# Second feed-forward product by seven half products, with the gated products parked in device memory

## The chip, the cores and the metric

The kernel runs on one core of one Trainium2 chip. The metric is device microseconds of one execution, and a smaller number is better. The engines are named as in the profile: PE is TensorE (matmuls), DVE is VectorE, ACT is ScalarE, POOL is GpSimd, and SP is SyncE, whose queue issues nearly all transfers. SBUF is the core's memory, PSUM holds matmul results in eight banks, and device memory is outside the core.

## What is computed

The reference is causal attention over 4 batches, 12 heads, 448 positions and 64 dimensions; then a layer with 4 attention experts of which each position mixes two; then a feed-forward block with a convolution gate. The last one is what the change touches:

```
h = np.maximum(x @ w_in, 0.0)                     # 4 x 448 x 1024
conv_out = sum over k of conv_w[k] * h shifted by k - 1
gate = 1.0 / (1.0 + np.exp(-conv_out))
return (h * gate) @ w_out                         # w_out: 1024 x 768
```

All values are float32.

## The kernel before

The feature dimension lies on the 128 partitions and the 448 positions of a batch lie in a row. A product keeps float32 accuracy by splitting both operands into a high part and the rest (a low part) and adding three passes: high x high, high x low, low x high (`PASSES`, line 24). So each operand of a product costs a copy (high) and a subtraction (low) ahead of it.

The program is written as tasks with needs, buffers and alternative engines (`Program.add`, line 135). `ORDER` (line 28) is a packed table: for each step it gives a task's number and the engine that runs it. `Program.run` (line 191) walks that table, so the table sets the order of the instructions on each engine. Where the table's planner expected PE to wait for long, `warm` (line 1314) puts small matmuls on the identity.

Four stages follow one another and overlap. `attend` (line 561) makes the first attention by pairs of heads (tiles `sk_A`, `P_A`, `PT_A`) and writes `xT` (lines 786 to 798). `proj_qk` and `proj_v` (lines 937 and 983) project it for the experts, and `attend` runs again with names in M. Both write `oc` to device memory (line 779). Meanwhile `fold_all` (line 834) folds the experts' output weights into w_in, giving `wp`, and `wout_convert` (line 1090) takes w_out, which comes as raw 64-bit words, to float32 (`from_f64`, line 395) and splits it: twelve steps of 512 columns, whose parts are saved to device memory.

`ffn_batch` (line 1145) loads `oc` of one batch, splits it on POOL (lines 1161 to 1171), and runs, for each of 8 chunks of 128 features, the first product (line 1188, 6 matmuls), relu on ACT (1201), three taps of the convolution (ACT at 1207, DVE at 1209 twice), tanh on ACT (1215), the gate's product on DVE (1219), and the split of the result into high (ACT, 1223) and low (DVE, 1226). The result stays in PSUM until it is split, and the parts `g` stay in SBUF.

`ffn_out` (line 1240) makes one block of 128 output features of one batch: 8 chunks x 3 matmuls (line 1251) into one bank, one evacuation by ACT or DVE (1261) and one store (1265). There are 6 blocks and 4 batches. A block may begin as soon as its batch's first chunks are split.

Of the kernel before, what the change touches and what calls it, by code (L numbers as in the profile page):

```python
# [33 lines left out]
    "z#{}aj)uF%q3{Ge4G$7N5&)u(2ofLTpWsXQCHxwG1OFG{Gl5Hlh(&M(d;z`$H^E)-5d4#}PoWa7!4KdC;VS_`nTTHEG37_n6OtO7BfTJP;kWTd"
    "0!(-dZW7DH3eiFE5)`Nm;hcyjT@nw7zfs;&b|@A60sa{OE9n(!gY=G6A)S*BNB|ioQi*+p5Mh9D1S)HEH6w&cLV*w>evi_k?8Fo?OT16KBt0aK"
    "5w3|-gd)LQGea(s$50${9yN^u$tA)NY8Leq^BHr1I6<5tZj$GTFPJZx+r%Rxo<t*YNEVWwq$16drKIP?CGsBmh$JRIA(qLDgjIrpZDc#x=aehT"
    "GLcGNA>L9BnODqX<~2z{M#zL(sFqfH!*r4&q<&J4lp=Xa+vFAUKDkIfCfmtCjh{Wv&a=<R%WPCFTzkr7*M1@6DFt?v>?d2uY4RX>i2R!QhFNB!"
    "DRb-vc9}iJUS%V-rrJ>LI5|&VXK%CrC5({9NO@A0{GM5;U9O$0y(7~pY>K_sS+i9uq39@k?1S2!+5>hG^@V*@yIQ+myHM+^F;Nth7(2th$0pQ#"
# [79 lines left out]
class Program:  # L118
# [64 lines left out]
    def idle_bank(self, since):  # L183

        for kinds in self.banks.values():
            for k in kinds:
                o = self.owner.get(k)
                if o is None or (o.left == 0 and o.ready <= since):
                    return k
# [75 lines left out]
def attn_moe_ffn_kernel(  # L265
# [1119 lines left out]
```

## Time and profile before

| | |
|---|---|
| median of 3 runs | 504.17 us (500.73 to 504.58) |
| the profiled execution's own time | 503.03 us |
| its span, first to last instruction | 501.2 us |
| PE, DVE, ACT, POOL busy | 97%, 74%, 70%, 52% of the span |
| matmul instructions in the page | 3202 |
| moved by DMA | 73.03 MB, 146 GB/s on average |

The page gives the busy time of each engine over the span. How busy an engine was in a stage is read from the table of stretches, what ended the wait of an engine from the table of waits, and what stands one behind the other up to the end from the chain. The duration of one instruction is in the groups by line and shape; matmul durations overlap with their neighbours, so the time from one matmul to the next is taken from the chain.

### The profile page before, as it was taken

Reading aid. Unit: us, or ns where it says so; the run is one execution under the profiler, and the core shown is the slowest. Engines: PE = TensorE matmul, PEld = TensorE weight load, DVE = VectorE, ACT = ScalarE, POOL = GpSimd, SP = SyncE. Lnnn points to the kernel's source line nnn. Section 1 sums busy time; section 2 is a strip of 40 time slices with the busy share of each in tenths; the row PEclk is TensorE's granted clock in tenths of the full one; section 3 lists DMA queues with packets and bytes.
Section 4 is the critical chain, followed back from the end, with each engine's and each line's share of the span. In section 5 each row is a group of like instructions: output and inputs, shape, how many; then the busy total and the mean of one; then the engine's idle time right before and its main releaser. Section 6 shows DMA issues by size and latency. Waiting matters only on the chain.

```text
span 501.2 us, 9905 instructions
## 1 busy us (share of the span) xinstructions
PE 487.5 (97%) x3202; PEld 419.7 (84%) x3202; DVE 369.0 (74%) x1110; ACT 349.8 (70%) x970; POOL 261.9 (52%) x388
## 2 busy tenths in 40 slices
PE   8788999999999999999999999999999999999997
PEld 6656878988888898888988788898999989999996
DVE  4999999988899686987789984487587556374300
ACT  5989999998889768886888893386566554344201
POOL 1856879978879777998788944162022002000000
PEclk9999999999999999999999999999999999999999
DMA  8857468996793767665688615838220112101011
GB/s 216 211 164 186 128 179 225 232 250 192 203 242 106 178 173 214 142 176 136 202 204 237 151 57 168 272 148 213 88 90 0 56 37 80 51 16 58 37 38 73
DMA packets 29171, 73.03 MB, mean 146 GB/s; under 512 B 4160, under 2 KB 11072, under 8 KB 28352
## 3 DMA queue, kind: packets, MB, share of 16 engines
q1 hardware_dynamic: 29040, 72.18, 51.8%
q8 instruction: 25, 0.41, 0.4%
q10 hardware_dynamic: 80, 0.23, 0.2%
q14 instruction: 26, 0.21, 0.1%
HBM read 50.50 MB, written 13.63 MB: 128 GB/s over the span
## 4 chain that ended last, share of the span: by engine, by line
PE 74%; DVE 11%; POOL 5%; DMA 4%; issue 2%; ACT 1%; SPq 0%; POOLq 0%; DVEq 0%; ACTq 0%
PE bank L1251 23%; PE bank L952 9%; PE bank L690 9%; PE bank L760 9%; PE bank L637 9%; PE bank L1188 8%; PE bank L998 4%; DMA nat<-in_qk_dram 4%; DVE P_A L650 3%; PE bank L881 3%; POOL sk_A L340 2%; DVE PT_A L337 1%; POOL P_M L333 1%; POOL P_A L333 1%; DMA cwraw<-in_conv_w_dram 1%
## 5 line engine op out<-in xcount | busy, mean ns | idle before, releaser
L1251 PE MATMUL bank<-g,wout 128*128 128x448 f32 x576 | 123.2, 367 | 0.0
L1251 PEld LDWEIGHTS bank<-g,wout 128*128 128x128 f32 x576 | 107.4, 188 | 8.8
L659 ACT ACTIVATE P_A<-P_A,nm_A 112x448 f32<-112x448 f32 (+3 forms) x192 | 99.4, 521 | 15.7 <-DVE nm_A L650 10.4
L340 POOL TENSOR_TENSOR sk_A<-nat,sk_A 64x448 fp32r<-64x448 f32 (+1 forms) x77 | 90.3, 1172 | 9.7 <-ACT sk_A L331 3.9
L650 DVE CUSTOM_DVE_ANT_0 P_A<-bank,mask 112x448 f32<-112x448 f32 (+3 forms) x192 | 80.0, 440 | 10.8 <-PE bank L595 6.3
L637 PE MATMUL bank<-sk_A 128*112 128x112 f32 (+3 forms) x352 | 66.4, 312 | 3.5 <-DVE nm_A L650 2.9
L952 PE MATMUL bank<-xT,wqk 128*128 128x448 f32 x288 | 68.7, 374 | 0.6 <-DVE sk_M L968 0.4
L690 PE MATMUL bank<-ident,P_A 112*112 112x112 f32 x480 | 61.7, 264 | 3.3 <-DVE xT L792 1.4
L333 POOL TENSOR_SCALAR P_A<-P_A,r_A 112x336 f32<-112x336 f32 (+3 forms) x97 | 49.9, 526 | 25.7 <-DVE r_A L670 9.2
L637 PEld LDWEIGHTS bank<-sk_A 128*112 128x112 f32 x352 | 48.8, 176 | 10.1 <-DVE nm_A L650 4.5
L690 PEld LDWEIGHTS bank<-ident,P_A 112*112 112x112 f32 x480 | 49.8, 135 | 8.0 <-DVE xT L792 1.6
L952 PEld LDWEIGHTS bank<-xT,wqk 128*128 128x128 f32 x288 | 51.2, 188 | 4.1 <-DVE sk_M L968 0.5
L1209 DVE SCALAR_TENSOR_TENSOR bank<-h,cw,bank 128x448 f32<-128x448 f32 x64 | 43.5, 687 | 14.8 <-ACT bank L1207 11.6
L760 PE MATMUL bank<-PT_A,v 112*64 112x448 f32 (+3 forms) x384 | 50.4, 406 | 0.1
L760 PEld LDWEIGHTS bank<-PT_A,v 112*64 112x64 f32 x384 | 26.2, 137 | 23.6 <-issue 12.3
L331 ACT ACTIVATE P_A<-P_A,r_A 112x448 f32<-112x448 f32 (+3 forms) x87 | 42.3, 517 | 4.6 <-DVE r_A L670 4.3
L1188 PE MATMUL bank<-ocs,wp 128*128 128x448 f32 x192 | 43.5, 367 | 0.0
L998 PE MATMUL bank<-wvg,xT 128*112 128x260 f32 x288 | 41.2, 287 | 0.2 <-DVE wm L434 0.2
L333 POOL TENSOR_SCALAR sk_A<-nat 128x896 fp32r<-128x896 f32 x35 | 33.0, 941 | 12.6 <-DMA nat<-in_qk_dram 11.6
L1188 PEld LDWEIGHTS bank<-ocs,wp 128*128 128x128 f32 x192 | 35.7, 188 | 3.0
L659 ACT ACTIVATE P_M<-P_M,nm_M 112x224 f32<-112x224 f32 (+3 forms) x64 | 33.3, 522 | 6.8 <-DVE nm_M L650 5.3
L331 ACT ACTIVATE PT_A<-bank 112x336 f32<-112x336 f32 (+1 forms) x75 | 33.9, 472 | 5.2 <-PE bank L690 5.0
(105 smaller groups left out, 820.2 us busy)
## 6 DMA issues: line engine op xcount, KB each, us to landing
nat<-in_qk_dram SPq DMA_DIRECT2D x88, 224.0 KB, 4.0
wraw<-in_w_in_dram SPq DMA_DIRECT2D x12, 512.0 KB, 5.5
woraw<-in_w_out_dram SPq DMA_DIRECT2D x12, 512.0 KB, 5.1
wo<-wohl SPq DMA_DIRECT2D x12, 512.0 KB, 4.1
wout<-wo SPq DMA_DIRECT2D x6, 1024.0 KB, 10.0
v<-in_v_dram SPq DMA_DIRECT2D x24, 224.0 KB, 4.5
out_dram<-osb SPq DMA_DIRECT2D x24, 224.0 KB, 1.9
sk_M<-sk_M SPq DMA_DIRECT2D x16, 224.0 KB, 4.2
```

Of the source, the lines that this page charges most:

```text
L331: nc.scalar.activation(dst, src, AF.Copy, scale=scale)
L333: nc.gpsimd.tensor_scalar(dst, src, scale, 1.0 if scale2 is None else scale2, ALU.mult, ALU.mult)
L340: (nc.gpsimd if e == "POOL" else nc.vector).tensor_tensor(dst, a, b, op)
L637: nc.tensor.matmul(sp[:CP], t[:, j.o[h], m * CP : (m + 1) * CP], t[:, j.o[h] + k, :w], start=(k == 2), stop=(k == 1),)
L650: nc.vector.tensor_tensor_reduce(rows(i), st["s", i][:CP, :w], mask[:, S - w :], -SCALE, 3.0e38, ALU.add, ALU.min, st["nm"][:, i : i + 1],)
L659: nc.scalar.activation(rows(i), rows(i), AF.Exp, bias=st["nm"][:, i : i + 1], scale=-1.0, accum_out=st["sm"][:, i, 0:1],)
L690: nc.tensor.transpose(pt[:CP, o : o + CP], rows(i)[:, kt * CP : (kt + 1) * CP], ident[:CP, :CP])
L760: nc.tensor.matmul(st["ov"][h * D : (h + 1) * D, kt * CP : S], j.v[:, kt, h, :], j.PT[h][:, col_base[kt] : col_base[kt] + S - kt * CP], st ...
L952: nc.tensor.matmul(st["ps"][:, :S], proj["wqk"][:, a, cc, w, p * P : (p + 1) * P], xT[b, cc][:, b2, :], start=(cc == 0 and (a, b2) == PASS ...
L998: nc.tensor.matmul(st[i][:CP, :VW], xT[b, cc][:, a, i * CP : (i + 1) * CP], proj["wvg"][:, b2, cc, :], start=(cc == 0 and (a, b2) == PASSE ...
L1188: nc.tensor.matmul(st["ps", c][:, :S], wp[:, a, ec, c * P : (c + 1) * P], st["oc", ec][:, b2], start=(ec == 0 and (a, b2) == PASSES[0]), s ...
L1251: nc.tensor.matmul(st["ps"][:, :S], ffn["wout", n][:, a, c], gs[c][:, b2], start=(c == 0 and (a, b2) == PASSES[0]), stop=(c == NFC - 1 and ...
```

## The change

Two batches are treated as the two halves of columns of one product, the two halves of w_out's rows (4 chunks each) and of its output features (3 blocks each) are the other halves, and the 2 x 2 half product is made with seven half products in place of eight. What changes in the code:

- `wout_convert` takes six steps, each with a block of w_out's upper and of its lower output half. It makes four sums and differences (`combine`), and saves seven sets of split half-size weights. `wset_load` loads them, 1.5 MB each.
- `ffn_batch` no longer splits the gated product. DVE writes it to SBUF in float32 (`mul`), and `park` stores it to device memory. The factor of one half of the gate goes into relu.
- `chunk_operands` loads the two chunks of a half of both batches of a pair back, makes four differences, and splits seven operands into high and low parts, on the engine that the table names.
- `ffn_out` runs once for a pair of batches: seven products of 3 blocks x 4 chunks x 3 matmuls. `ffn_sum` adds each result to what `SUMS` names: a running sum in SBUF or a quarter of the output, which is then stored.
- The space comes from tiles that the attention leaves (`unit_space`, `HOMES`): names that begin with `ux`, `us`, `uv`, `up` and `uq` are such tiles; "u" slots hold split operands, "w" slots loaded chunks, "d" slots differences and running sums.
- `ORDER` is a new table for the whole program.

```diff
-    BANKS = dict(s=(0, 1, 4), t=(2, 3, 5), v=(4, 5), m=(6, 7), h=(6, 7, 0, 2), o=(5, 3, 1))
+    BANKS = dict(
+        s=(0, 1, 4), t=(2, 3, 5), v=(4, 5), m=(6, 7), h=(6, 7, 0, 2), o=(5, 3, 1, 4, 2, 0),
...
+    PRODUCTS = ((0, "b11"), (1, "b21"), (2, "t2"), (4, "t3"), (5, "t1"), (3, "b22"), (6, "t4"))
...
+            n = k * FW
+            th = add(either("whi", 0, {"ACT": act_sb(n), "DVE": 60 + 0.54 * n}), 0, hi, need, take=[whl], free=frees)
+            tl = add(either("wlo", 0, of_two(n)), 0, lo, [th], free=frees)
...
+        a22 = parts(lambda: vals[1]()[:, 1:2], 1, 6, [vals[1, "t"]])
+        s1 = combine(at(1, 1), at(1, 0), at(1, 1), ALU.add, a22)
+        up = parts(lambda: vals[0](), 2, 0, [vals[0, "t"]])
+        s3 = combine(at(1, 0), at(0, 0), at(1, 0), ALU.subtract, s1 + [vals[0, "t"]])
+        parts(lambda: vals[1](), 2, 4, s3, wms[1:])
+        s2 = combine(at(0, 0), at(1, 1), at(0, 0), ALU.subtract, s3 + up)
+        s4 = combine(at(0, 1), at(0, 1), at(0, 0), ALU.subtract, s2)
+        parts(lambda: vals[0](), 2, 2, s4, wms[:1])
...
-                nc.scalar.activation(st[c][:, 1 : S + 1], st["ps", c][:, :S], AF.Relu)
+                nc.scalar.activation(st[c][:, 1 : S + 1], st["ps", c][:, :S], AF.Relu, scale=0.5)
...
+            def park(c=c):
+                nc.sync.dma_start(g_d[b, c % HC][:, c // HC], st["g", c])
...
-            t = add("DVE", dve(S), mul, [t], free=[hb])
-            t = add("ACT", act_ps(S), g_hi, [t])
-            gd[c] = add("DVE", dve(S), g_lo, [t], free=[mb])
+            t = add("DVE", dve(S), mul, [t], take=[gb], free=[hb, mb])
+            parked[b, c] = add("SP", dma(224), park, [t], free=[gb], lag=2100)
...
+            loads.append(add("SP", dma(448), load, [parked[b, c2], parked[b, c2 + HC]], take=[fs[y]], lag=LAND))
...
+        b11 = parts("b11", x[0, 0], loads[:1], fs[:1])
+        b21 = parts("b21", x[0, 1], loads[:1], fs[:1])
+        t1 = sub(1, x[0, 0], x[1, 0], x[0, 0], loads[1:] + b11, free=fs)
+        t3 = sub(1, x[1, 0], x[1, 1], x[1, 0], t1, free=fs[1:])
+        t2 = sub(1, lambda: unit(tb), x[1, 1], x[0, 0], t1, take=[tb], free=fs)
+        t4 = sub(1, x[0, 1], x[0, 1], lambda: unit(tb), t2 + b21, free=[tb, fs[0]])
...
+    SUMS = (
+        (("s", None),),
+        (("c11", "s"),),
+        (("u", "s"),),
+        (("s", "u"),),
+        (("c22", "s"), ("u", "u")),
+        (("c12", "u"),),
+        (("c21", "s"),),
+    )
...
+                    t = add(
+                        "PE", mm(S, 3), part(c2), dep + wset_done[s] + [t],
+                        take=[] if c2 else [pb], free=[ub],
                     )
...
+        if src:
+            r = add("DVE", dve(S), partial(go, "DVE"), need, take=take, free=free)
```

How the new table moves instructions, at three places. First PE, where the second product begins. Before, at the transposes of the last batch's first expert job (`P_M3_0`; L690 transposes, L1188 first product, L1251 second product):

```order
L1188 MATMUL bank0_61<-ocs_0_0_4317,wp_97 128x448 x3
L1188 MATMUL bank0_61<-ocs_0_1_4318,wp_97 128x448 x3
L690 MATMUL bank5_66<-ident_71,P_M3_0_0_4435 112x112 x3
L690 MATMUL bank3_64<-ident_71,P_M3_0_0_4435 112x112 x3
L1251 MATMUL bank1_62<-g_0_0_4501,wout0_4650 128x448 x3
L1251 MATMUL bank1_62<-g_0_1_4459,wout0_4650 128x448 x3
L1251 MATMUL bank3_64<-g_0_0_4501,wout1_4667 128x448 x3
L1251 MATMUL bank3_64<-g_0_1_4459,wout1_4667 128x448 x3
L1251 MATMUL bank5_66<-g_0_0_4501,wout2_4652 128x448 x3
L1251 MATMUL bank5_66<-g_0_1_4459,wout2_4652 128x448 x3
```

and after, at the same transposes (L718 transposes, L1323 first product, L665 scores, L1563 identity):

```order
L1323 MATMUL bank6_67<-ux_0_4300,wp_97 128x448 x3
L1323 MATMUL bank6_67<-ux_1_4301,wp_97 128x448 x3
L718 MATMUL bank3_64<-ident_71,P_M3_0_1_4539 112x112 x4
L1563 MATMUL bank1_62<-ident_71 128x128 x4
L665 MATMUL bank4_65<-sk1_M3_1_4634 112x448 x2
L665 MATMUL bank1_62<-sk1_M3_1_4634 112x224 x2
L665 MATMUL bank1_62<-sk1_M3_1_4634 112x112 x2
L718 MATMUL bank5_66<-ident_71,P_M3_0_0_4574 112x112 x4
L718 MATMUL bank2_63<-ident_71,P_M3_0_1_4539 112x112 x3
L665 MATMUL bank0_61<-sk1_M3_1_4634 112x336 x2
L718 MATMUL bank3_64<-ident_71,P_M3_0_0_4574 112x112 x3
L1563 MATMUL bank1_62<-ident_71 128x128 x2
```

Before, second-product matmuls of batch 0 stand directly behind these transposes. After, the scores of the last job (`sk1_M3_1`) and matmuls on the identity do, and the first matmul of the second product (L1456) is 36 rows further from the first of these rows, behind four more pairs of first-product rows.

Second DVE, in the middle of the first product. Before (L1209 taps, L1219 gate's product, L1226 low part):

```order
L1209 SCALAR_TENSOR_TENSOR bank0_61<-h_1_5_5025,cw_96,bank0_61 128x448 x2
L1219 SCALAR_TENSOR_TENSOR bank2_63<-bank2_63,h_2_3_5016 128x448
L1226 TENSOR_TENSOR g_2_3_5086<-bank2_63,g_2_3_5086 128x448
L1219 SCALAR_TENSOR_TENSOR bank0_61<-bank0_61,h_1_5_5025 128x448
L1226 TENSOR_TENSOR g_1_5_5128<-bank0_61,g_1_5_5128 128x448
L1209 SCALAR_TENSOR_TENSOR bank7_68<-h_2_1_5045,cw_96,bank7_68 128x448 x2
L337 TENSOR_SCALAR PT_M3_1_1_0_5058<-bank3_64 112x336
L1209 SCALAR_TENSOR_TENSOR bank6_67<-h_2_0_5053,cw_96,bank6_67 128x448 x2
L1219 SCALAR_TENSOR_TENSOR bank7_68<-bank7_68,h_2_1_5045 128x448
L1226 TENSOR_TENSOR g_2_1_5200<-bank7_68,g_2_1_5200 128x448
```

and after (L1344 taps, L1354 gate's product, L356 and L359 the helpers for one and two inputs):

```order
L1344 SCALAR_TENSOR_TENSOR bank0_61<-h_2_0_5063,cw_96,bank0_61 128x448
L1354 SCALAR_TENSOR_TENSOR g_1_6_5107<-bank7_68,h_1_6_5024 128x448
L359 TENSOR_TENSOR ux_0_4300<-ux_6_4783,ux_0_4300 128x448
L1344 SCALAR_TENSOR_TENSOR bank0_61<-h_2_0_5063,cw_96,bank0_61 128x448
L1354 SCALAR_TENSOR_TENSOR g_2_0_5125<-bank0_61,h_2_0_5063 128x448
L356 TENSOR_SCALAR ux_2_4361<-bank1_62 128x448
L359 TENSOR_TENSOR ux_2_4361<-uq_1_4846,ux_6_4783 128x448
L356 TENSOR_SCALAR up_0_4973<-uq_0_4845 128x448
L359 TENSOR_TENSOR up_0_4973<-uq_0_4845,up_0_4973 128x448
L1344 SCALAR_TENSOR_TENSOR bank6_67<-h_2_3_5082,cw_96,bank6_67 128x448 x2
L359 TENSOR_TENSOR up_3_5019<-ux_7_4784,up_3_5019 128x448
L359 TENSOR_TENSOR ux_7_4784<-uq_2_4971,ux_7_4784 128x448
```

The low part out of PSUM is gone. Between the taps now stand differences and low parts of operands, which read SBUF (`ux`, `uq`), and evacuations of products.

Third SP's queue, where the last batch's expert keys are stacked. Before (L492 and L500 stack, L1157 loads `oc`, L1128 loads a weight block, L1266 stores output):

```order
L1157 DMA ocs_1_0_4700<-oc_1_0_102 128x448
L1157 DMA ocs_1_1_4701<-oc_1_1_103 128x448
L1128 DMA wout5_4754<-wo_5_113 128x2048
L500 DMA sk0_M3_1_4492<-sk0_M3_1_4492 64x448
L500 DMA sk0_M3_1_4492<-sk0_M3_1_4492 64x896
L1128 DMA wout4_4758<-wo_4_112 128x2048
L1266 DMA out_0_dram<-osb_0_0_4819 128x448
L1157 DMA ocs_2_0_4868<-oc_2_0_104 128x448
```

and after (L1299 loads `oc`, L1357 parks a chunk, L1389 loads a parked pair):

```order
L1299 DMA ux_1_4301<-oc_1_1_103 128x448
L1357 DMA g_0_0_109<-g_0_4_4706 128x448
L1357 DMA g_0_3_112<-g_0_7_4693 128x448
L1357 DMA g_0_2_111<-g_0_6_4779 128x448
L1389 DMA ux_6_4783<-g_0_0_109 128x896
L1299 DMA us_0_4828<-oc_2_0_104 128x448
L1389 DMA ux_7_4784<-g_0_3_112 128x896
L1357 DMA g_0_1_110<-g_0_5_4826 128x448
L1389 DMA ux_8_4835<-g_0_2_111 128x896
L1357 DMA g_1_0_113<-g_1_4_4849 128x448
L1299 DMA us_0_4828<-oc_2_1_105 128x448
L1389 DMA uq_0_4845<-g_0_1_110 128x896
```

Before, weight blocks and `oc` loads stand there. After, the parks of batch 0's chunks and their loads alternate with the `oc` loads of later batches, each load behind the park that it needs.

## Rows read from the trace of the kernel before

**Rows 1.** the page: PE busy us (share) and count; GB/s in 40 slices
```profile
...
PE 487.5 (97%) x3202; PEld 419.7 (84%) x3202; DVE 369.0 (74%) x1110; ACT 349.8 (70%) x970; POOL 261.9 (52%) x388
...
GB/s 216 211 164 186 128 179 225 232 250 192 203 242 106 178 173 214 142 176 136 202 204 237 151 57 168 272 148 213 88 90 0 56 37 80 51 16 58 37 38 73
```

**Rows 2.** stretches, busy us: PE PEld DVE ACT POOL; clock, DMA, GB/s
```profile
...
0.00:50.00 50.00, 42.17 (x266) 31.22 (x266) 42.01 (x143) 40.82 (x123) 27.88 (x39) 0.97 0.75 194
50.00:300.00 250.00, 247.73 (x1870) 210.86 (x1870) 220.96 (x754) 214.88 (x643) 204.91 (x273) 1.00 0.68 182
300.00:501.00 201.00, 197.57 (x1068) 177.65 (x1066) 106.00 (x216) 94.06 (x205) 29.13 (x77) 1.00 0.28 89
```

**Rows 3.** the chain of waits from 440 us: start us, us, what
```profile
...
461.70 35.88 PE bank L1251 x177
...
497.65 0.54 ACT osb L331
```

**Rows 4.** groups of PE: count | busy us, mean ns | idle before
```profile
...
L1251 PE MATMUL bank<-g,wout 128*128 128x448 f32 x576 | 123.2, 367 | 0.0
```

**Rows 5.** waits of PE, first and last of twelve: us, times, longest
```profile
...
PE bank L637 <- DVE nm_A L650: 3.3, 4, 1.9
...
PE bank L998 <- DVE wm L434: 0.2, 1, 0.2
```

**Rows 6.** groups of DVE by shape, columns as in rows 4
```profile
...
L1209 DVE SCALAR_TENSOR_TENSOR bank<-h,cw,bank 128x448 f32<-128x448 f32 x64 | 43.5, 687 | 14.8 <-ACT bank L1207 11.6 <-POOL ocs L1163 1.9 <-issue 0.5
...
L1219 DVE SCALAR_TENSOR_TENSOR bank<-bank,h 128x448 f32<-128x448 f32 x32 | 19.9, 628 | 7.9 <-ACT bank L1215 7.6
L1226 DVE TENSOR_TENSOR g<-bank,g 128x448 fp32r<-128x448 f32 x32 | 19.8, 621 | 18.4 <-ACT g L1223 18.3
...
L340 DVE TENSOR_TENSOR sk_A<-nat,sk_A 128x448 fp32r<-128x448 f32 x9 | 7.7, 851 | 0.7 <-ACT sk_A L331 0.7
...
L929 DVE TENSOR_TENSOR wvg<-praw,wvg 128x260 fp32r<-128x260 f32 x6 | 5.4, 894 | 0.0
...
L929 DVE TENSOR_TENSOR wqk<-praw,wqk 128x512 fp32r<-128x512 f32 x6 | 5.1, 854 | 0.4 <-ACT wqk L925 0.4
...
L337 DVE TENSOR_SCALAR P_A<-P_A,r_A 112x448 f32<-112x448 f32 x2 | 1.4, 676 | 0.0
```

**Rows 7.** line L792: ns min/median/max, first and last start us
```profile
...
L792 DVE TENSOR_TENSOR xT<-bank,xT x24: 585/621/625, 36.5 to 304.9; 128x448 fp32r<-128x448 f32 x24
```

**Rows 8.** PE in order of time from 327 us: start us, us, what
```profile
...
327.75 0.47 PE L637 MATMUL bank<-sk_M 128*112 128x336 f32 x2
...
336.56 0.83 PE L690 MATMUL bank<-ident,P_M 112*112 112x112 f32 x7
```

**Rows 9.** DMA issues: count, KB each, median us to landing
```profile
...
nat<-in_qk_dram SPq DMA_DIRECT2D x88, 224.0 KB, 4.0
...
wout<-wo SPq DMA_DIRECT2D x6, 1024.0 KB, 10.0
...
oc<-oc SPq DMA_DIRECT2D x8, 224.0 KB, 3.3
```

**Rows 10.** groups of POOL by shape, columns as in rows 4
```profile
...
L1108 POOL TENSOR_TENSOR wohl<-wm,wohl 128x512 fp32r<-128x512 f32 x12 | 15.4, 1289 | 3.4 <-ACT wohl L1105 2.4 <-POOL sk_A L340 0.9
...
L1169 POOL TENSOR_TENSOR ocs<-ocs 128x448 fp32r<-128x448 f32 x8 | 9.3, 1157 | 0.4
...
L1163 POOL TENSOR_SCALAR ocs<-ocs 128x448 fp32r<-128x448 f32 x8 | 4.6, 569 | 45.6 <-DMA ocs<-oc 45.6
```

**Rows 11.** groups of ACT by shape, columns as in rows 4
```profile
...
L1207 ACT ACTIVATE bank<-h,cw 128x448 f32<-128x448 f32 x32 | 20.2, 638 | 0.6
...
L1223 ACT ACTIVATE g<-bank 128x448 fp32r<-128x448 f32 x32 | 17.3, 543 | 11.4 <-DVE bank L1219 11.0
...
L331 ACT ACTIVATE P_A<-P_A,r_A 112x448 f32<-112x448 f32 x23 | 15.1, 661 | 1.9 <-DVE r_A L670 1.9
```

**Rows 12.** line L340 on DVE: ns min/median/max, first and last start us
```profile
...
L340 DVE TENSOR_TENSOR sk_A<-nat,sk_A x11: 606/623/1570, 30.5 to 164.3; 128x448 fp32r<-128x448 f32 x9, 64x448 fp32r<-64x448 f32 x2
```

More of the change, by code (lines that the diff above doesn't have):

```diff
@@ L1 @@
 from contextlib import ExitStack
+from functools import partial
 import base64
@@ L34 @@
[L34 to L38, printed above, removed]
@@ L187, in idle_bank @@
                 o = self.owner.get(k)
-                if o is None or (o.left == 0 and o.ready <= since):
+                if k < 8 and (o is None or (o.left == 0 and o.ready <= since)):
                     return k
@@ L393, in attn_moe_ffn_kernel, with from_f64 @@
     open_pool("w", "right")
-    def from_f64(raw, raw_buf, load, shape, n, need=(), take=()):
+    def from_f64(raw, raw_buf, load, shape, n, need=(), take=(), own=None):
         st = {}
@@ L434, in flush @@
             nc.vector.scalar_tensor_tensor(m, m, 2.0**-30, view(st["ps"]), ALU.is_ge, ALU.mult)
-        ts = add("ACT", act_sb(n) + 35, square, [load], take=[sq], free=[raw_buf])
-        t = add("DVE", dve(n), bits, [load, *need], take=[mb, *take])
+        ts = add("ACT", act_sb(n) + 35, square, [load, *need], take=own[0] if own else [sq], free=[raw_buf])
+        t = add("DVE", dve(n), bits, [ts], take=[mb, *take])
         t = add("DVE", dve(n), top, [t])
@@ L616, in pair_scores @@
         j.taken = [j.scored[NQ - 1]]
+        j.began += j.taken
     def head(j, h, moe):
@@ new lines, in ffn_sum, with go, store @@
+    def ffn_sum(q, turn, m, st, tmp, t, pb, dst, src):
+        last = st.setdefault("last", {})
+        need = [t, last.get(("w", src, m)), last.get(("w", dst, m))] + last.get(("r", dst, m), [])
+        take, free = [], [pb]
+        if src:
+            free.append(tmp[src, m])
+        ob = None
+        if dst in QUARTERS:
+            ob = Buf("osb")
+            take = [ob]
+        elif ("w", dst, m) not in last:
+            take = [tmp[dst, m]]
+        def go(e):
+            acc = ps(pb)[:, :S]
+            if dst in QUARTERS:
+                w = st[dst, m] = pools["a"].tile([P, S], F32, tag="osb", name=f"osb_{q}_{dst}_{m}", bufs=RINGS["osb"])
+            else:
+                w = unit(tmp[dst, m])
+            if src:
+                nc.vector.tensor_tensor(w, acc, unit(tmp[src, m]), ALU.add)
+            else:
+                copy(e, w, acc)
+        if src:
+            r = add("DVE", dve(S), partial(go, "DVE"), need, take=take, free=free)
+        else:
+            r = add(either("osb", q, {"DVE": dve(S), "ACT": act_ps(S)}), 0, go, need, take=take, free=free)
+        last["w", dst, m] = r
+        last.setdefault(("r", src, m), []).append(r)
+        if dst in QUARTERS:
+            n0, y = QUARTERS[dst]
+            def store():
+                nc.sync.dma_start(out[:, n0 + m, 2 * q + y], st[dst, m])
+            add("SP", 800, store, [r], free=[ob], lag=3200)
```

465 lines of the change are left out of this document (293 added, 172 removed).

## The prediction

> **What bounds the kernel now.** I read the page's busy times first, then busy time by stretches of the span, then the chain of waits, then the groups by shape. The page says that TensorE (PE) is busy for 97% of the span [rows 1]. The stretches show where this holds: in the first 50 us PE, DVE and ACT are each busy for about 42 us, so nothing is saturated and all wait for each other; from 50 to 300 us PE is busy for 247.7 of 250 us, with DVE at 221, ACT at 215 and POOL at 205; from 300 us on PE is busy for 197.6 of 201 us, and that gap is the tail after the last product [rows 2]. There DVE has 95 us to spare, ACT 107 and POOL 172. The granted clock is 1.00 from 50 us on, the upper of the two levels. A busy PE need not be PE at its peak, so I checked the pitch: in the last stretch of the chain 177 matmuls of the second feed-forward product follow one another in 35.88 us, 202.7 ns each, and nothing stands between them [rows 3]. The 367 ns that the group shows for one such matmul is its own duration, with neighbours overlapping [rows 4]. So the second half of the program is a queue of matmuls at a fixed pitch: a matmul taken away there is worth its pitch, as long as the operands of those left come in time. All waits of PE that the profile finds are twelve entries of 9.7 us together, from 3.3 down to 0.2 us [rows 5].
>
> **The products.** Before, each batch takes 6 blocks of rows x 8 chunks x 3 passes = 144 matmuls, 576 in all. After, each pair of batches takes 7 products x 3 blocks x 4 chunks x 3 passes = 252, 504 in all. 72 matmuls fewer at 202.7 ns are 14.6 us. The shape of each (128x128 against 128x448) stays. The 192 first-product matmuls, and all of the attention, stay.
>
> **The weights.** Six steps now make seven half-size weight sets out of w_out, with four sums or differences each, where twelve steps only split the weights into a high and a low part. In the orders the high parts go from twelve 512-wide on ACT to five on ACT and thirteen on DVE, with six 256-wide ones beside them; the low parts from twelve 512-wide on POOL to eleven on POOL and seven on DVE, with six 256-wide ones; the combinations are 24 256-wide ones, 16 on POOL and 8 on DVE. With 0.85 us for a 512-wide and 0.89 for a 256-wide two-input operation on DVE, and 0.68 for a copy [rows 6], DVE gets some 27 us more. The order gives part of it on: 19 evacuations of transposes and 14 normalisations of the first attention move to ACT. I counted the rows ahead of the last tile of the attention's output (before, the last of its 24 low parts starts at 304.9 us [rows 7]), each at its form's mean: DVE 13.5 us more, ACT 19 us more, POOL 2 us less; PE has the same work there within 3 us. The idle time of DVE and ACT from 50 to 300 us is 29 and 35 us [rows 2], so it fits, but at 93 to 95% busy. The order also moves the folding of w_in forward: 132 of its 144 matmuls now stand ahead of the last product of the first batch's attention, none did. That loads DVE where it is full already and relieves it later; PE had waits there to fill. Bounds: nothing, if the idle time takes it all; 19 us, if ACT's addition lies on the path. PE at 99% beside engines at 86 to 88% says that the order hides such work well, so I take a value near the lower end, 4 us, with 10 as the upper end that I believe.
>
> **The entrance to the second product.** Before, the first chunks of batch 0 feed its 6 blocks straight away, and the products fill PE's queue while the last attention jobs wait for their softmax. After, the first product needs batch 0's chunks parked, loaded again as pairs and split. Its first matmul stands behind all of batch 0's first product and most of batch 1's. Ahead of it lie the last scores, transposes and 24 first-product matmuls of batch 1. Two waits can open. The last head's softmax took from 328.2 to 336.6 us, 8.3 us, from its last score to its first transpose [rows 8]; after, what stands between for the second job is 9 transposes, 8 scores and 24 matmuls, some 7 us: 1.4 us short. The parked chunk: relu, taps and tanh some 3 us with 2 us of ACT's queue ahead, product 0.63, store 3.3, load of twice 224 KB about 4.0 (nearest: one nat load), high 0.57, low 1.16 [rows 6, 9 to 11]: 14.4 us against 36 first-product matmuls, 27 transposes, 16 scores and a value product behind its own matmuls, some 14 us. Behind this load on SP's queue stand the next parks and loads, so a late one delays the later chunks too. Bounds 0 and 9 us (three such waits of 3 us); I take 3.
>
> **Operands and sums in the second half.** Added: 96 two-input operations instead of 40 low parts (48 on DVE, 48 on POOL), 64 copies instead of 40 (30 ACT, 23 POOL, 11 DVE), 42 additions out of PSUM on DVE and 6 copies, instead of 24 evacuations. At 0.85 for a DVE operation from SBUF, 0.62 from PSUM, 1.16 and 0.57 on POOL and 0.66 on ACT [rows 6, 10, 11]: DVE 48 x 0.85 + 11 x 0.62 + 43 x 0.62 less 43 x 0.62 that go = +47 us, POOL +55, ACT -2. DVE then has 153 us of work in a stretch of 186, POOL 84, ACT 92. PE's queue covers it: one product of 36 matmuls lasts 7.3 us and needs 4 high and 4 low parts and 3 to 6 sums, some 8 us on three engines. With less cover each of the 14 product starts would cost its low part's 1.2 us. I take 1 us, the upper end is the rival below. The last sum is on DVE (0.62) where ACT's 0.54 stood [rows 3], then a store: nothing.
>
> **Transfers.** 32 parks of 224 KB, 16 loads of 448 KB and 7 weight sets of 1.5 MB instead of 6 of 1.0: 19.4 MB more in 186 us, 104 GB/s on top of 89 [rows 2]. The page's slices show up to 250 GB/s [rows 1], so this fits. A 1.0 MB load took 10 us to land [rows 9], a 1.5 MB one 15 by that; the last three sets are issued well ahead of their first use. Nothing for them.
>
> **Sum.** 503.0 us (span 501.2, 1.8 around it; 0.2% under the median of 504.17) - 14.6 + 4 + 3 + 1 = 496.4, say 496.
>
> **A rule that speaks against it.** DVE's two-input operation on SBUF operands has a median of 623 ns but a mean of 851 over nine and a maximum of 1570, which is nearly the median plus one of POOL's 1.15 us operations [rows 6, 12]; from PSUM it is 621 [rows 6]. So some of them waited for POOL. The Trainium skill says this outright (GPSIMD Engine Reference, section 8, Key points): POOL shares its SBUF interfaces with VectorE, and contends with DVE instructions that have two SBUF inputs. By that rule, the trace agrees. In rows: at the median's 0.62 DVE has 142 us to do in 186 and the sum stays; at the maximum for each of them the sum is that of the last rival.
>
> **The rivals.**
> 1. Forecast: the saving less some 8 us of new waits, 491 to 499, 496. Chance 0.45.
> 2. All of it hides: 503.0 - 14.6 = 488.4, or 486 if the reordered attention gains 2. For it: PE's idle is 3.4 us in 201 now. Against: the chain from chunk to product is 14 us longer. 0.22.
> 3. The attention stage stretches: ACT gets 19 us more on 215 of 250, DVE 13.5 on 221. If half of ACT's addition shows, +10: 499 to 504. For it: in the first 50 us PE waits as it is. Against: 99% from 50 us on. 0.18.
> 4. The parked chunks come late at each product: 14 starts at 1 us more on top of the forecast's waits: some 505. For it: SP's queue is in order, and a store stands in it until its product is done. Against: between the last chunk of a pair and the first product that needs the second batch stand some 17 to 22 us of matmuls. 0.08.
> 5. Slower: DVE and POOL hold each other up in the second half. If each of the 48 operations waited for a POOL operation, they cost 48 x 1.57 = 75 us instead of 41, DVE has 187 us to do in 186 and becomes the bound, and POOL waits in turn; with the dependences between them some 10 us more than now, 513. It decides from DVE at about 180 us. For it: the maximum [rows 12]. Against: by the median, more than half of them were not held up. 0.07.
>
> **How the numbers follow.** About 1% is what a measurement of this kernel can tell from no change, since the three runs lie between 500.7 and 504.6. 1% under the median is 499.1: cases 1 and 2 lie below it, 0.67; a little of case 1 above it and of case 3 below cancel. Within 1%: cases 3 and 4, 0.26. Slower: 0.07. The range leaves out the slower case, the lowest end of case 2 and the top of case 4: 487 to 505. The likeliest case alone is 491 to 499.
>
> **What would show it.** In the profile after: 504 matmuls in the second product at 203 ns in the chain; PE at 99% from 50 to 300 us and the last tile of the attention's output at 305 to 315 us; PE idle of 2 to 6 us between the last scores and the first second-product matmuls; DVE at 150 us of busy time or less after that, POOL at 80 to 90; waits of PE for the operand tiles under 3 us in all. The forecast is wrong if the attention stage ends 10 us later, if PE waits for operands at each product, or if the DVE operations on SBUF operands have a mean of 1.2 us or more.

## The result, and the profile after

The changed kernel takes 497.88 us, the median of six runs (495.83 to 498.41), beside 503.49 us of the kernel before on the same chip: a ratio of 0.988, with a 95% interval of 0.985 to 0.992. Four more runs with the experiments below gave 0.990 (0.985 to 0.995). The profiled execution took 498.41 us, with a span of 496.6 us, 4.6 us less than the 501.2 us of before. The forecast was 496.0 in 487 to 505, and faster by over 1%; the ratio is 1.2% below one, and its interval reaches from 0.8% to 1.5%. The 72 matmuls alone would have given 14.6 us.

The page's busy times of the changed kernel, as in [rows 1]:

```profile
PE 477.4 (96%) x3142; PEld 405.5 (82%) x3142; DVE 414.4 (83%) x1183; ACT 360.2 (73%) x996; POOL 322.7 (65%) x441
```

PE is busy for 10.1 us less, DVE for 45 and POOL for 61 us more. By stretches, columns as in [rows 2]:

```profile
0.00:50.00 50.00, 42.74 (x283) 32.65 (x284) 40.99 (x139) 42.52 (x123) 35.23 (x50) 1.00 0.77 220
50.00:300.00 250.00, 242.44 (x1808) 200.82 (x1807) 228.33 (x758) 222.30 (x665) 195.96 (x253) 1.00 0.71 195
300.00:496.60 196.60, 192.20 (x1056) 172.03 (x1054) 145.09 (x288) 95.35 (x212) 91.56 (x139) 1.00 0.57 191
```

From 50 to 300 us PE now stands idle for 7.6 us where it did for 2.3. From 300 us on DVE has 145 us of work and POOL 92, forecast as 153 and 84, and PE's idle time there is 4.4 us where it was 3.4. The chain of waits of the second product (start, us, what; its line is now L1456) answers to [rows 3]:

```profile
395.51 9.76 PE bank L1456 x48
...
432.42 60.66 PE bank L1456 x297
```

297 matmuls in 60.66 us are 204 ns each, with nothing between them. The line that writes the attention's output (L821, [rows 7]), ns min/median/max, first and last start us:

```profile
L821 DVE TENSOR_TENSOR xT<-bank,xT x24: 593/621/625, 37.0 to 308.9; 128x448 fp32r<-128x448 f32 x24
```

The last of them comes 4.0 us later than before. PE's waits, the first three of 17 and one from further down, as in [rows 5]:

```profile
PE bank L718 <- ACT PT_A L350: 2.9, 3, 1.9
PE bank L665 <- DVE nm_A L678: 2.8, 5, 1.0
PE bank L718 <- DVE xT L821: 1.8, 2, 1.2
...
PE bank L665 <- DMA sk_M<-sk_M: 0.5, 1, 0.5
```

All 17 together are 15.7 us, before they were 9.7. L1456 is in none of them: by this view the second product never waits for its operands.

**Where the saving went.** PE's busy time and its waits do not tell it, since a busy PE need not be at its pitch. So I counted the matmuls that PE had done by a given time, line by line, and weighted each kind with its pitch. The pitches come from PE in order of time, such as these rows of the changed kernel (start us, us from the first start to the last end, what):

```profile
61.07 1.59 PE L910 MATMUL bank<-whl,woT 128*128 128x256 f32 x12
62.50 1.12 PE L718 MATMUL bank<-ident,P_A 112*112 112x112 f32 x10
92.23 4.51 PE L1027 MATMUL bank<-wvg,xT 128*112 128x260 f32 x36
...
102.01 7.44 PE L981 MATMUL bank<-xT,wqk 128*128 128x448 f32 x36
```

Less the last one's own 0.37 us (the group's mean), 36 projections take 7.07 us, 202 ns from one to the next; in the same way a folding matmul and one of the value projection take 121 ns, a transposition 96. For scores and value products I took 135 and 125 ns, means over their four widths. The matmuls that only fill PE's queue count nothing. Such a count is good to about 1 us: the changed kernel twice differs by that much, and the run of the kernel before with fewer matmuls, told of below, whose work is the same up to the second product, is 0.6 us ahead of it at 100 us and within 0.3 from 200 to 340. The table gives how far each kernel is behind the kernel before, in us of matmuls; those in the lower rows are told of below.

| kernel | at 100 us | 200 | 300 | 340 | 360 | 380 |
|---|---|---|---|---|---|---|
| changed kernel | 4.4 | 4.5 | 6.4 | 6.3 | 9.4 | 9.7 |
| changed kernel again | 4.5 | 5.3 | 7.6 | 7.5 | 10.3 | 10.9 |
| its w_in without DVE's steps | 0.1 | 0.2 | 2.2 | 2.1 | 5.2 | 5.3 |
| its weight sets without sums | 3.8 | 3.1 | 4.0 | 3.8 | 6.8 | 7.3 |
| chunk pairs loaded without a wait | 3.2 | 3.1 | 5.4 | 5.3 | 8.4 | 8.5 |
| last stacking without a wait | 2.7 | 3.4 | 5.7 | 5.8 | 8.9 | 9.1 |
| new order, w_in spread out | 0.8 | 3.3 | 7.3 | 8.3 | 11.4 | 11.4 |
| new order, w_in early | 1.3 | 5.8 | 8.7 | 8.2 | 11.1 | 12.1 |
| kernel before, w_in without DVE's steps | 3.1 ahead | 4.1 ahead | 4.0 ahead | 4.4 ahead | 4.1 ahead | 4.3 ahead |

So 14.6 us less of matmuls, 6.4 us lost by 300 us and 3.1 us between 340 and 360; at 380 us the kernel is 9.7 behind, 4.9 ahead on balance, and from there on both run at their pitch. The profiled spans differ by 4.6.

### The profile page after: what moved, and what is told of

Its sections match the earlier page's. It is cut to its first block, busy times and chain, and to the rows that moved or that the text cites. A ratio compares the mean times of both kernels' runs of the same rounds, so it can differ in the third digit from the quotient of the medians.

```text
span 496.6 us, 10098 instructions
## 1 busy us (share of the span) xinstructions
PE 477.4 (96%) x3142; PEld 405.5 (82%) x3142; DVE 414.4 (83%) x1183; ACT 360.2 (73%) x996; POOL 322.7 (65%) x441
## 4 chain that ended last, share of the span: by engine, by line
PE 67%; ACT 13%; DVE 9%; POOL 4%; issue 3%; DMA 3%; SPq 0%; POOLq 0%; DVEq 0%; ACTq 0%
PE bank L1456 21%; PE bank L789 10%; PE bank L665 8%; PE bank L981 8%; PE bank L1323 7%; PE bank L718 7%; ACT P_A L687 5%; PE bank L1027 4%; DVE P_A L678 2%; ACT PT_A L350 2%; ACT P_A L350 2%; DMA wraw<-in_w_in_dram 1%; POOL sk_A L359 1%; DMA wset<-wohl 1%; PE bank L1563 1%
## 5 line engine op out<-in xcount | busy, mean ns | idle before, releaser
L359 POOL TENSOR_TENSOR sk_A<-nat,sk_A 64x448 fp32r<-64x448 f32 (+1 forms) x76 | 90.4, 1190 | 15.2 <-ACT sk_A L350 7.7
L665 PE MATMUL bank<-sk_A 128*112 128x336 f32 (+3 forms) x352 | 65.0, 310 | 4.8 <-DVE nm_A L678 2.8
L718 PE MATMUL bank<-ident,P_A 112*112 112x112 f32 x480 | 59.8, 261 | 5.3 <-ACT PT_A L350 2.9
L665 PEld LDWEIGHTS bank<-sk_A 128*112 128x112 f32 x352 | 48.7, 175 | 13.8 <-DVE nm_A L678 5.7
L718 PEld LDWEIGHTS bank<-ident,P_A 112*112 112x112 f32 x480 | 48.6, 133 | 10.1 <-ACT PT_A L350 3.4
L350 ACT ACTIVATE P_A<-P_A,r_A 112x336 f32<-112x336 f32 (+3 forms) x101 | 50.6, 530 | 4.6 <-DVE r_A L698 4.6
L352 POOL TENSOR_SCALAR P_A<-P_A,r_A 112x448 f32<-112x448 f32 (+3 forms) x83 | 43.5, 534 | 16.0 <-DVE r_A L698 6.8
L1456 PE MATMUL bank<-up,ws 128*128 128x448 f32 x225 | 52.8, 366 | 0.0
L1344 DVE SCALAR_TENSOR_TENSOR bank<-h,cw,bank 128x448 f32<-128x448 f32 x64 | 43.1, 685 | 7.7 <-ACT bank L1342 4.7
L350 ACT ACTIVATE PT_A<-bank 112x336 f32<-112x336 f32 (+1 forms) x94 | 42.7, 477 | 4.2 <-PE bank L718 4.1
L789 PEld LDWEIGHTS bank<-PT_A,v 112*64 112x64 f32 x384 | 25.4, 136 | 24.9 <-issue 12.1
L1456 PEld LDWEIGHTS bank<-up,ws 128*128 128x128 f32 x225 | 42.2, 188 | 3.8
L1456 PE MATMUL bank<-us,ws 128*128 128x448 f32 x180 | 43.8, 367 | 0.0
L352 POOL TENSOR_SCALAR P_M<-P_M,r_M,g_w 112x224 f32<-112x224 f32 (+3 forms) x54 | 32.0, 601 | 10.0 <-DVE r_M L698 5.1
L352 POOL TENSOR_SCALAR sk_A<-nat 128x896 fp32r<-128x896 f32 x30 | 28.7, 956 | 14.3 <-DMA nat<-in_qk_dram 13.7
L687 ACT ACTIVATION_READ_ACCUMULATOR P_A<-P_A,nm_A 112x1 f32 x192 | 37.6, 196 | 0.0
```

What stands on the lines that cost most here:

```text
L350: nc.scalar.activation(dst, src, AF.Copy, scale=scale)
L352: nc.gpsimd.tensor_scalar(dst, src, scale, 1.0 if scale2 is None else scale2, ALU.mult, ALU.mult)
L359: (nc.gpsimd if e == "POOL" else nc.vector).tensor_tensor(dst, a, b, op)
L665: nc.tensor.matmul(sp[:CP], t[:, j.o[h], m * CP : (m + 1) * CP], t[:, j.o[h] + k, :w], start=(k == 2), stop=(k == 1),)
L687: nc.scalar.activation(rows(i), rows(i), AF.Exp, bias=st["nm"][:, i : i + 1], scale=-1.0, accum_out=st["sm"][:, i, 0:1],)
L718: nc.tensor.transpose(pt[:CP, o : o + CP], rows(i)[:, kt * CP : (kt + 1) * CP], ident[:CP, :CP])
```

## The experiments

Ratios are to runs of the kernel before on the same chip; us are medians. 1% is 5 us.

### The matmuls alone

The kernel before, without the last of eight chunks in each block of the second product:

```diff
-                for a, b2 in PASSES:
+                for a, b2 in PASSES if c < NFC - 1 else ():
...
-                        stop=(c == NFC - 1 and (a, b2) == PASSES[2]),
+                        stop=(c == NFC - 2 and (a, b2) == PASSES[2]),
```

> The kernel before, with the eighth chunk of every block of the second product left out: 504 matmuls in place of 576, nothing else changed. Theory A (the second half of the kernel before is a queue of matmuls at a fixed pitch): 72 x 202.7 ns = 14.6 us less, 488.9 us, within 1.5 us. Rival: where DVE, ACT or the stores of the output set the end, a part of it stays, and the time is above 492 us.

489.93 us, 0.974 (0.970 to 0.978): 13.2 us less, profiled span 488.2, 13.0 less, within the 1.5 us of theory A. Of the missing 1.6 us by the spans, 1.3 stand in its chain of waits (start us, us, what):

```profile
452.65 7.31 PE bank L1251 x36
...
459.99 0.64 DVE osb L337
...
477.46 0.64 DVE osb L337
```

Twice PE waits for an evacuation on DVE, 0.64 us each, which the chain of the kernel before with its longer blocks does not have. The pitch holds: a matmul taken out of this queue is worth what it takes there.

### DVE's steps on w_in left out

The order of the changed kernel has all 144 folding matmuls of w_in ahead of 100 us, the one before 36 (busy us and count of that line from 0 to 100 us, clock, DMA, GB/s; the kernel before):

```profile
0.00:100.00 100.00, 4.90 (x36) 0.98 0.74 192
```

and the changed kernel:

```profile
0.00:100.00 100.00, 19.42 (x144) 1.00 0.72 211
```

In exchange it has done 24 scores, 47 transpositions, 32 value products and all of 36 projections of q and k less, and 13 value projections more. My first theory (A) was that this order costs what is lost by 100 us, because a piece of w_in takes four DVE steps of 0.69 us and DVE is full there. I left the four steps out, in both kernels (their w_in is then another number):

```diff
-        t = add("DVE", dve(n), bits, [ts], take=[mb, *take])
+        t = add("DVE", dve(n), bits if not light else (lambda: None), [ts], take=[mb, *take])
```

and so for the other three.

> The kernel before, with the four DVE steps that turn a double of w_in into a float left out for each of the 12 pieces (48 operations of 0.69 us, 33 us of DVE work); the high and low parts and the folding matmuls stay. Their pieces are loaded between 40 and 240 us here. Theory A (PE waits for DVE in the first 100 us alone, and only 3 of the 12 pieces stand there in this kernel): 1 to 3 us less, 500.5 to 502.5 us. Rival B (DVE's load from 100 to 300 us costs PE time too): 5 us less or more, below 498.5 us.

> The changed kernel, with the same four DVE steps of w_in left out for each of the 12 pieces. Here all 12 stand ahead of 92 us, in a stretch where DVE is busy for 98% from 20 to 80 us. Theory A (of the 14.6 us that the 72 matmuls give, some 8 are lost in the first 100 us, because these 33 us of DVE work stand where DVE is the engine that all wait for): 6 to 10 us less than the changed kernel, 488 to 492 us. Theory B (the loss is the work of the weight sets from 60 to 300 us): 0 to 2 us less, 496 to 498. Theory C (the loss is at the entrance to the second product): no change, 497 to 498.5.

Before: 499.57 us, 0.995 (0.992 to 0.999), 2.4 us less: the 1 to 3 of theory A, not the 5 of rival B. Changed: 494.91 us, 0.984 (0.980 to 0.989), 2 us under the changed kernel's 0.988, with intervals that overlap; in the profiled spans 492.2 to 496.6, 4.4 less, and in the table 4.3 less lost by 100 us. That is half of what A wanted for this kernel.

The 4.0 us that the kernel before gains in the table are not all of the cut. By the same count 2.4 of them are there at 50 us, and the first of the steps that were left out starts at 52.3 us (the line of the first step in the kernel before, ns min/median/max, first and last start us):

```profile
L422 DVE TENSOR_SCALAR bank<-wraw x12: 681/690/701, 52.3 to 253.0; 128x512 int32<-128x512 int32 x12
```

So the two profiles differ ahead of the edit; from 20 to 30 us the granted clock was 0.83 in the one of the kernel before and 1.00 in the other. That leaves 1.6 us, and the time says 2.4 (0.7 to 4.1 by the interval). So these runs do not show that DVE's early load is a special price of the new order: 33 us less DVE work are worth 2.4 us in the kernel before and 2 to 4 in the changed one. DVE is short in both: from 20 to 100 us it is busy for 78.7 of 80 us before and 78.0 after. Busy us of PE, PEld, DVE, ACT and POOL from 20 to 100 us show what comes next. The changed kernel:

```profile
20.00:100.00 80.00, 69.07 (x536) 56.50 (x535) 78.02 (x220) 73.26 (x204) 64.95 (x69) 1.00 0.73 211
```

and without the DVE steps:

```profile
20.00:100.00 80.00, 73.82 (x561) 62.28 (x562) 53.95 (x180) 75.45 (x215) 65.57 (x69) 0.98 0.80 222
```

DVE falls from 98% to 67%, PE gains 4.7 us, and ACT at 94% is then the busiest of the three that feed it.

### The sums of halves of w_out left out

```diff
-        return [add(either("wadd", 0, of_two(FW)), 0, lambda e: two(e, dst(), a(), b2(), op), need)]
+        return [add(either("wadd", 0, of_two(FW)), 0, lambda e: None, need)]
```

> The changed kernel, with the 24 sums and differences of halves of w_out left out (8 on DVE, 16 on POOL, 256 wide), so that every weight set is split from an uncombined half; all else stays. Theory A: 0 to 1 us less, 497 to 498. Theory B (the weight sets' added work from 60 to 300 us holds PE up): 3 us less or more, below 495. Theory C: no change.

495.68 us, 0.986 (0.982 to 0.991); the time alone does not tell this from the changed kernel. The profiled span is 493.9, 2.7 less, and the table shows the difference between 100 and 300 us: 4.0 lost by 300 us where four profiles with the sums have 5.4 to 7.6. So 24 short operations of the weight sets cost some 2 us, more than A and less than B expected; with four profiles that spread over 2.2 us, the size is good to about 1 us.

### The entrance to the second product

> The changed kernel once more, unchanged, beside the next three, so that differences of 1 to 3 us can be told. Every theory: 0.988 of the kernel before, within 0.004.

> The changed kernel; the 16 loads of chunk pairs read a stretch of the weight sets in device memory, of the same size and shape, that was written before 300 us, so no load waits for a parked chunk (the products are then of other numbers). The parks stay. Counted by matmuls done, the changed kernel falls 3.2 us behind between 340 and 360 us. Theory E (that is the round trip of the parked chunks): 2 to 3.5 us less than the changed kernel. Theory F (it is the last projected attention job: projection, stacking by transfers, scores, softmax): no change, within 0.7 us.

> The changed kernel; the five transfers that stack the operands of the last projected attention job read early device memory in place of the projection's result (its scores are then of other numbers), so the scores of one of its two heads no longer wait for the projection and its evacuation. Theory F: 1 to 3 us less than the changed kernel, with the filling matmuls at 347 to 352 us gone. Theory E: no change, within 0.7 us.

```diff
-                nc.sync.dma_start(unit(fs[y]), g_d[b, c2])
+                nc.sync.dma_start(unit(fs[y]), wset_d[:, 0, :, 0, 0, :S])
```

for the first and

```diff
-                nc.sync.dma_start(f(dst), f(src))
+                nc.sync.dma_start(f(dst), far if early else f(src))
```

for the second, in `stack`, where `early` is the job of the last batch and pair and `far` a piece of `wset_d` of the same shape. 0.990 unchanged, 0.991 (0.988 to 0.994) without the wait for parks, 0.992 (0.988 to 0.995) without the wait for the projection: no gain from either, and both lose the same 3.1 us between 340 and 360. E and F both fall as waits that could be named. The first edit takes away only the wait for the parks to land, which in the changed kernel holds SP's queue for 1.5 us from 335 to 400 us (us, times, longest); the loads still stand behind the parks in that queue:

```profile
SPq L1389 <- DMA g<-g: 1.5, 2, 1.0
```

The trace of the changed kernel settles the rest. The low part that the first matmul of the second product needs is done on POOL at 359.5 us, and PE comes to that matmul 1.9 us later, straight from a value product (start us, us, what):

```profile
358.34 1.14 POOL L359 TENSOR_TENSOR us<-ux,us 128x448 fp32r<-128x448 f32 x1
...
359.38 2.11 PE L789 MATMUL bank<-PT_M,vm 112*64 112x448 f32 x16
...
361.42 0.88 PE L1456 MATMUL bank<-us,ws 128*128 128x448 f32 x3
```

PE in order of time in the run without the wait for the projection, whose lines stand two further down (start us, us, what):

```profile
345.67 0.55 PE L720 MATMUL bank<-ident,P_M 112*112 112x112 f32 x4
346.05 1.07 PE L1565 MATMUL bank<-ident 128*128 128x128 f32 x8
346.88 1.02 PE L667 MATMUL bank<-sk_M 128*112 128x448 f32 x6
...
350.11 0.62 PE L1565 MATMUL bank<-ident 128*128 128x128 f32 x4
...
360.50 0.87 PE L1458 MATMUL bank<-us,ws 128*128 128x448 f32 x3
```

The wait for the stacking is gone, and the 12 filling matmuls (L1565) are there as before. The first matmul of the second product comes at 360.5 us; the kernel before had done 54 of them by 360, and they stood between its last scores and transpositions, the first two groups of them here:

```profile
342.10 3.89 PE L1251 MATMUL bank<-g,wout 128*128 128x448 f32 x18
...
346.24 3.20 PE L1251 MATMUL bank<-g,wout 128*128 128x448 f32 x15
```

Busy us of PE, PEld, DVE, ACT and POOL in the changed kernel:

```profile
345.00:350.00 5.00, 4.52 (x35) 4.15 (x33) 4.89 (x11) 4.04 (x8) 1.21 (x4) 1.00 0.83 194
350.00:355.00 5.00, 4.62 (x33) 3.91 (x31) 4.97 (x18) 4.96 (x17) 1.14 (x1) 1.00 0.84 265
```

DVE, then ACT too, are full: the last softmax shares them with the taps and the multiplication of the first product. PE, whose work is in a fixed order, has no second product to fill with. The chain of waits of the changed kernel agrees: from 343.2 to 351.9 us it runs on ACT and DVE, through the taps, the gate's product and the last softmax (start us, us, what):

```profile
344.50 0.70 DVE bank L1344
345.23 1.29 DVE bank L1344 x2
...
347.14 0.62 DVE g L1354
...
350.64 0.83 ACT P_M L687 x4
```

But the load of these 10 us itself was not taken away, so this is the reading that is left, not a shown cause.

### The second half's slack

Each low part of the second product's operands computed twice, first on both engines, then on one:

```diff
-                two(e, unit(ub)[:, 1], ap(), f(unit(ub)[:, 0]), ALU.subtract)
+                for _ in range(2 if e == "DVE" else 1):
+                    two(e, unit(ub)[:, 1], ap(), f(unit(ub)[:, 0]), ALU.subtract)
```

> The changed kernel, with each of the 56 low parts of the second product's operands computed twice: 24 more operations on DVE at 0.7 to 0.9 us, 32 more on POOL at 1.2 to 1.5. DVE then has some 163 us of work in the second half's 187, POOL some 133. Theory A (a queue of matmuls at a fixed pitch, the operands made well ahead): less than 1.5 us more. Rival (DVE and POOL hold each other up, rival 5 of the prediction, not far from its point): 6 us more or above.

> The changed kernel, with the 24 low parts of the second product's operands that DVE computes done twice (0.62 us each undisturbed, 15 us), those on POOL once. With all 56 doubled the kernel took 529 us, 32 more. Theory G (the two engines slow each other where both work on operands from SBUF, and the price is set by how long POOL is busy): 2 to 8 us more than the changed kernel. Theory H (DVE's own queue is what the operands wait for): 15 us more or above.

> The changed kernel, with the 32 low parts that POOL computes done twice (1.15 us each undisturbed, 37 us), those on DVE once. Theory G: 20 to 30 us more than the changed kernel, with DVE's operations on SBUF operands above a mean of 0.9 us (0.76 in the changed kernel). Theory H: 8 us more or less, since POOL stands idle for half of the second half of the changed kernel (92 of 187 us are busy).

Both: 529.29 us, 1.054 (1.049 to 1.058), 32 us above the changed kernel by the ratios (0.989 of 503, the mean of its ten runs). DVE's 24: 510.40 us, 1.015 (1.009 to 1.021), 13.3 more. POOL's 32: 511.71 us, 1.017 (1.012 to 1.023), 14.5 more. By the profiled spans it is 30.9, 12.2 and 12.3 us. Theory A falls, and neither G nor H fits: each engine costs 12 to 14 us, and both together more than the sum. Line L359 (operations with two operands from SBUF) from 300 us to the end, busy us and count on DVE, then on POOL: the changed kernel,

```profile
300.00:496.62 196.62, 36.69 (x48) 59.07 (x49) 1.00 0.57 191
```

DVE's doubled,

```profile
300.00:508.80 208.80, 58.13 (x72) 60.64 (x49) 0.99 0.54 179
```

POOL's doubled,

```profile
300.00:508.90 208.90, 41.60 (x48) 99.06 (x81) 0.98 0.53 176
```

and both.

```profile
300.00:527.53 227.53, 66.53 (x72) 101.72 (x81) 0.97 0.48 161
```

21.4 us more on DVE cost 13.3, 40.0 us more on POOL cost 14.5. Now the second product (here L1457) does wait, for the doubled operands among others. PE's largest waits for them (us, times, longest), with DVE's doubled,

```profile
PE bank L1457 <- DVE us L359: 1.8, 3, 0.8
```

and with POOL's:

```profile
PE bank L1457 <- POOL up L359: 6.3, 6, 2.1
```

In the changed kernel the stretches of 20 us after the entrance are (PE, PEld, DVE, ACT, POOL):

```profile
360.00:380.00 20.00, 20.00 (x116) 16.44 (x113) 17.97 (x31) 16.41 (x33) 13.72 (x26) 1.00 0.65 224
380.00:400.00 20.00, 20.00 (x99) 18.36 (x98) 18.55 (x29) 12.32 (x25) 8.91 (x13) 1.00 0.84 307
400.00:420.00 20.00, 20.00 (x99) 18.22 (x99) 17.71 (x30) 7.96 (x15) 11.07 (x14) 1.00 0.57 209
```

and with DVE's low parts doubled:

```profile
380.00:400.00 20.00, 18.25 (x86) 15.33 (x85) 18.83 (x31) 10.79 (x21) 7.03 (x10) 1.00 0.73 255
400.00:420.00 20.00, 16.93 (x81) 14.70 (x80) 18.27 (x28) 8.52 (x16) 12.32 (x15) 1.00 0.45 164
```

DVE is at 89 to 93% from 360 to 420 us, where the first product's taps run beside the operands; its mean of 74% over the second half hid that. PE loses nothing there as the kernel stands. With DVE's low parts doubled PE stands idle for 8.5 us from 360 to 500 us, 4.8 of them in these two stretches from 380 to 420.

### Where w_in stands

If no engine has room in the attention stage, the loss should move with the order and not go away. Two new orders of the same operations, one with w_in spread over the stage (36 of its 144 matmuls done by 100 us), one with it early (132 by 100 us). Only the list of operations that sets the order and the engines is another.

> The changed kernel, the same work in another order: the conversions of the projection weights first, the 12 pieces of w_in spread over the attention stage (near 45 to 250 us, as in the kernel before), the six steps on w_out between them; 391 of the operations that may run on several engines are on another one. Theory A (the early place of w_in costs 4 us): at 100 us as many matmuls are done as in the kernel before, and the time is 3 to 5 us below that of the changed kernel, 493 to 495. Theory I (DVE and ACT have no room left for the weights' added work, wherever it stands): nothing is lost at 100 us, but the same 4 us are lost between 200 and 300, and the time is within 1.5 us of the changed kernel's.

> The control to the run with w_in spread out: a new order of the same work, of the same origin, that keeps the 12 pieces of w_in ahead of 90 us. 413 operations are on another engine than in the changed kernel. Theory A: as the changed kernel, within 1.5 us, with some 4 us of matmuls lost by 100 us. Theory I: the same time too, so that the two new orders do not differ by more than 1.5 us.

501.37 us, 0.998 (0.995 to 1.001), and 503.23 us, 1.003 (1.001 to 1.006). Neither is within 1.5 us of the changed kernel; both are slower, and no order here beats it. Spread out, 0.8 us are lost at 100 us, 3.3 at 200 and 7.3 at 300; early, 1.3, 5.8 and 8.7. In the changed kernel it is 4.4, 4.5 and 6.4. Theory A falls, and by its control too: that order has w_in early and loses 1.3 us by 100 us where A wanted 4. Theory I had the place of the loss right for the order that is spread out (4.0 us between 200 and 300) and the time wrong. What is borne out is that in all three orders 6 to 9 us are lost by 300 us, early or late; the place of w_in alone does not say when. The orders differ in much besides w_in (some 400 operations on another engine), so which move sets the place of the loss, and how much of their own extra loss lies with which, stays open.

## Why the prediction held, step by step

1. **The products.** 14.6 us by the pitch; the cut alone gave 13.2 (13.0 by the spans), with 1.3 of the rest found in two waits. In the changed kernel the last 297 of the 504 matmuls follow one another at 204 ns with no such wait. Right.
2. **The weights.** Forecast 4 us with 10 as the upper end; measured 6.4 by 300 us (5.4 to 7.6 in four profiles). Right in kind, too small by 2.4. The step took DVE's and ACT's idle time (29 and 35 us from 50 to 300 us) as room. But the kernel before gains 2.4 us (0.7 to 4.1) from 33 us less DVE work, so DVE was not as free as a PE at 99% made it look: all but 1.2 of its 29 us of idle time lie behind 100 us. At that rate, a fourteenth of a us for each us, the 13.5 that DVE got would cost 1.0 us (an estimate, 0.3 to 1.7 by the interval); what ACT's 19 us cost was not measured apart, and the split of the 6.4 stays open but for the 2 us of the sums. What the folding's early place does, which I thought would fill PE's waits, is open too: of two orders that have it, one loses 4.4 us by 100 us and the other 1.3.
3. **The entrance.** Forecast 3 us, measured 3.1, but from one of its two waits, so that the number agrees is partly luck. The parked chunk, on which I spent most of the working (its terms add up to 14.7 us, not 14.4), makes PE wait nowhere: the operand that was made from it lay ready 1.9 us ahead, and without the wait for the parks to land nothing changed. The other half (the last softmax is short of cover, 1.4 us by my count) has the right place and half the size.
4. **Operands and sums.** Forecast 1 us, measured none that the trace shows: PE is busy for every 20 us from 360 to 480. The busy times were right to within 8 us. What failed is the margin that I gave it: rival 5 should decide from DVE at 180 us, but at 145 plus 21 us it cost 13.3 us already. The step spread DVE's work evenly over 186 us.
5. **Transfers.** Nothing, as forecast. The load of a weight set, of which I put 15 us, landed sooner than the smaller one before ([rows 9]); issue, count, KB, median us to landing:

```profile
ws<-wset SPq DMA_DIRECT2D x7, 1536.0 KB, 7.6
```

6. **Sum.** 503.0 - 14.6 + 6.4 + 3.1 + 0 = 497.9, beside the profiled 498.4 and the median of 497.88. The forecast's 4 + 3 + 1 and the measured 6.4 + 3.1 + 0 agree to 1.5 us, partly by luck, since step 4's error and step 2's offset each other.
7. **Rival 5.** DVE and POOL did not hold each other up enough to matter here. DVE's operations with two operands from SBUF have a mean of 36.69 / 48 = 764 ns, 867 with POOL's doubled, 924 with both. The forecast's 850 was too high as the kernel stands, and the rival's 1.57 us, which single operations reach, was never near as a mean. The Trainium skill states that POOL shares its SBUF interfaces with VectorE (GPSIMD Engine Reference, section 8, Key points); these three means agree.

Of the signs named ahead, the pitch (203 ns, found 204), the last output tile (305 to 315 us, found 308.9), DVE (150 or less, 145) and the waits for operands (under 3 us, none) came out, and POOL at 92 is just above its 80 to 90. Two did not. PE at 99% from 50 to 300 us was 97%, which goes with step 2's missing 2.4 us. And PE idle for 2 to 6 us ahead of the second product was 0.9 us, from 345 to 355 us: most of the rest of the loss stands under filling matmuls (1.7 us), where idle time does not show it.

## What to carry to other kernels

A matmul removed from a queue that runs at its pitch is worth its pitch; what prepares its operands is paid for in the stage where it is put, and an engine that is 98% busy for a part of that stage is not free there, even where its mean over the stage is 88% and PE is at 99%. Before calling an engine's slack in a stage, cut the stage into pieces of the length of its dependences: a mean of 74% hid 60 us at 90% at its start. To see where a saving went, count the matmuls done by a given time: three orders of the same work lost 6 to 9 us by the same point, each at another place. And look where in such a count a difference begins: 2.4 us of one stood there before its edit could act.

## What was not expected of the hardware

An operation on DVE with two operands from SBUF (128x448) takes 0.61 us at the least and up to 1.58 in the changed kernel's second half (POOL's 1.14 to 1.54), but the mean grows slowly with POOL's load: twice the low parts on POOL add 103 ns to the mean of DVE's. TensorE's granted clock, 1.00 from 300 to 480 us in the changed kernel, fell in single stretches where PE waited for doubled operands, to a mean between its two levels (1.2 and 2.4 GHz). With POOL's doubled (PE, PEld, DVE, ACT, POOL, clock):

```profile
460.00:480.00 20.00, 18.20 (x87) 15.77 (x87) 18.08 (x22) 2.31 (x4) 17.82 (x16) 1.00 0.07 24
480.00:494.00 14.00, 11.04 (x45) 9.41 (x44) 7.31 (x11) 0.58 (x1) 12.28 (x12) 0.84 0.13 49
```

The stretch of 0.84 follows one in which PE stood idle for 1.8 of 20 us, and it stands idle in 3.0 of the 14 itself. How much of the 14.5 us is the clock was not measured. A 1.5 MB load out of device memory landed in 7.6 us, where one of 1.0 MB took 10.0 in the kernel before; size alone does not tell it.
